# Two down products moved behind the first later unit's difference products, and differences made from the high part

## The chip, the cores and the metric

The kernel runs on one core of one Trainium2 chip. The metric is the device time of one execution in microseconds; of several runs the median is given. The engines are called TensorE (PE in the profile; PEld is its weight load), VectorE (DVE), ScalarE (ACT), GpSimd (POOL) and SyncE (SP, which here only issues DMAs).

## What is computed

The reference is an attention block with a polynomial sketch, followed by a gated feed-forward block:

```python
# 4 batches, 4 heads, 1088 positions, head size 32, sketches of 8
def phi(x):                                  # 64 features per position
    a = einsum('rd,bhsd->bhsr', S1, x); b = einsum('rd,bhsd->bhsr', S2, x)
    return einsum('bhsi,bhsj->bhsij', a, b).reshape(..., 64)
q_p, k_p = phi(q), phi(k)
kv  = einsum('bhsf,bhsd->bhfd', k_p, v);  z = k_p.sum(axis=2)
x   = einsum('bhsf,bhfd->bhsd', q_p, kv) / (einsum('bhsf,bhf->bhs', q_p, z) + 1e-6)
x   = x.transpose(0, 2, 1, 3).reshape(4352, 128)      # tokens x model width
g   = x @ w_gate;  val = x @ w_val                    # 128 x 1536 each
out = (g * sigmoid(g) * val) @ w_out                  # 1536 x 128
```

## The kernel before

**Blocks, units, downs.** The 4352 tokens are cut into blocks: three for batch 0 (384, 384 and 320 columns), then blocks of 480 and a last one of 384. The hidden width of 1536 is cut into twelve chunks of 128. A *unit* is one block and one chunk: its gate and value products, the SiLU and the product of the two, written to a slot of `hbuf` or `late`. A *down* product multiplies one such slot by a chunk of `w_out` and adds into the block's PSUM bank; after twelve of them the bank is transposed (L1117) and stored.

**Two kinds of units.** The three blocks of batch 0 (the *first batch*) use plain 32-bit products (L1027). The *later units*, numbered y = 0 to 83 in `line`, use a split: each operand is cut into a high part (`x1`, the number times `CUT`, rounded), a low part (`x0`, the number less `x1`) and a *difference* (`xd`), and three faster fp32r products take the place of the plain one. `start_unit(y)` issues the two difference products of a unit (L990, one for the gate, one for the value) into a pair of PSUM banks, and one ScalarE instruction that rescales both banks in place (L993). `finish_unit(y)` adds the high and the low products on top (L1003 and L1004, twice each), then ScalarE takes the SiLU (L1006) and VectorE the product (L1011), which frees the pair. There are three pairs. The loop starts unit y + 1 before it finishes unit y, so that a unit's L993 lies beside the products of the unit before; unit 0 is started ahead of the loop.

**The moving side's parts.** `cut_tokens` makes x1 on ScalarE (L882), x0 (L883, on VectorE for the first block and on GpSimd for the six others) and xd on VectorE (L887). `cut_hidden` does the same for the hidden side of 30 chosen down products, in three steps put into later units: the high part h1 at y + 1 (L965 or L967), the low part h0 on GpSimd at y + 2 (L968), the difference hd on VectorE at y + 3 (L971). In the kernel before, both differences are made from the low and the high part: high − 4096 × low.

```python
        nc.vector.scalar_tensor_tensor(
            out=xd[:, 0:n], in0=whole(x0[:, 0:n]), scalar=-BETA, in1=whole(x1[:, 0:n]),
            op0=ALU.mult, op1=ALU.add,
        )
```

The scales in L938 (the plain downs' weights where a block mixes both kinds), L993 and L1096 (the sum of a block's two banks) take the factor 4096 out again.

**Order.** Every engine works off its own instructions in the order in which the program issues them; the order round the change is written out by hand. After the units of batch 0 a loop issues the down products that are left in `todo`, three a turn, and between them pieces of the attention of the later batches (`parts_of`, which takes the next step of the generator `attentions`) and of the cutting of the gate weights (`take`). Then the first later block is cut, and the loop over the later units begins:

```python
    while todo:
        for _ in range(min(3, len(todo))):
            down()
        ...
        parts_of(1 + (begun[0] and len(todo) > 2))
    ...
    run(x_steps or cut_tokens(HEAD, nc.vector))
```

The attention pieces that follow are, one a unit, the transposes of k (L330, two) and of q (L581, two) on VectorE; the groups of small attention products on TensorE (L391, L357, L720, later L345, L783) are called by `group` at y = 4, 6, 20, 22 and 40. `bank()` hands out PSUM banks: by name, in turn, or, once `oldest` is set, the bank that was used longest ago.

Of the kernel before, what the change touches and what calls it, by code (L numbers as in the profile page):

```python
# [12 lines left out]
AF = mybir.ActivationFunctionType  # L13
ALU = mybir.AluOpType
# [5 lines left out]
def kernel(  # L20
# [28 lines left out]
    nc = tc.nc  # L49
# [42 lines left out]
    place = dict(g0=0, g1=1, g2=2, acc=3, a=4, b=6)  # L92
    used = {i: 0 for i in range(8)}
    held = set()
    oldest = [False]
    clock = [0]

    def touch(*which):
# [4 lines left out]
    def hold(*tags):  # L103
        for t in tags:
            held.update((place[t], place[t] + 1) if t in "ab" else (place[t],))
# [7 lines left out]
    def bank(tag=None):  # L113

        if tag is not None:
            i = place[tag]
        elif oldest[0]:
            i = min((i for i in used if i not in held), key=used.get)
        else:
            i = place[free_banks[turn[0] % len(free_banks)]]  # L120
            turn[0] += 1
        touch(i)
        return PS[:, i, :]
# [31 lines left out]
    wo = const.tile([P, NCH, D], FP32, name="wo")  # L155
# [32 lines left out]
    def load_next():  # L188
# [36 lines left out]
        out=ident[:], in_=ident[:], pattern=[[-1, P]], base=0, channel_multiplier=1,  # L225
# [79 lines left out]
    def run(*gens):  # L305
        for g in gens:
            for _ in g:
                pass
# [497 lines left out]
    acc = {}  # L806
    todo = []
# [6 lines left out]

    BETA = 4096.0
    CUT = 1.0 - 2.0**-13
    w_parts = {}
    x_parts = {}  # L820

    def whole(ap):
        return ap.bitcast(FP32)
# [17 lines left out]
    def cut_weights(w, lows, engine):  # L841
# [3 lines left out]
        for c, (w1, wb, wd) in enumerate(homes(w)):  # L845
# [4 lines left out]
            if engine is nc.vector:  # L850
                fine = dict(
                    out=wd, in0=low, scalar=-BETA, in1=whole(w1), op0=ALU.mult, op1=ALU.add
                ), engine.scalar_tensor_tensor
            for row, f, args in zip(
                rows,
                (nc.scalar.activation, engine.tensor_tensor, nc.scalar.activation, fine[1]),
                (
                    dict(out=w1, in_=src, func=AF.Copy, scale=CUT),
                    dict(out=low, in0=src, in1=whole(w1), **sub),
                    dict(out=wb, in_=low, func=AF.Copy, scale=BETA),  # L860
                    fine[0],
# [12 lines left out]
    def cut_tokens(i, engine=nc.gpsimd):  # L874

        t0, n = blocks[i]
        x = xT[:, t0 : t0 + n]
        x1, x0, xd = x_parts[i] = [
            apool.tile([P, WB], F32R, tag=tag, name=name, bufs=2)
            for tag, name in (("qb", "x1"), ("dT", "x0"), ("rd", "xd"))  # L880
        ]
        nc.scalar.activation(x1[:, 0:n], x, AF.Copy, scale=CUT)  # L882
        engine.tensor_tensor(  # L883
            out=x0[:, 0:n], in0=x, in1=whole(x1[:, 0:n]), op=ALU.subtract
        )
        yield
        nc.vector.scalar_tensor_tensor(  # L887
            out=xd[:, 0:n], in0=whole(x0[:, 0:n]), scalar=-BETA, in1=whole(x1[:, 0:n]),
            op0=ALU.mult, op1=ALU.add,
        )  # L890

# [7 lines left out]
    before, behind = {}, {}  # L901

    def add_to(where, y, f):
        where.setdefault(y, []).append(f)
# [5 lines left out]
    def cut_down():  # L910

        n = len(FINE)
        parts = const.tile([P, 3, n, D], F32R, tag="room", name="dparts", bufs=1)
        w1, wb, wd = (parts[:, k] for k in range(3))
        scaled = apool.tile([P, len(PLAIN), D], FP32, tag="zs", name="scaled")
        low = const.tile([P, n, D], FP32, tag="late", name="dlow", bufs=1)
        down_parts.update(w1=w1, wb=wb, wd=wd, scaled=scaled)
        rest = [(0, slice(0, 1)), (1, slice(1, 8, 2)), (5, slice(6, 7)), (6, slice(NCH - 1, NCH))]

        def high(c):  # L920
            nc.scalar.activation(w1[:, c], wo[:, FINE[0] :][:, c], AF.Copy, scale=CUT)

        def left(c):
            nc.gpsimd.tensor_tensor(
                out=low[:, c], in0=wo[:, FINE[0] :][:, c], in1=whole(w1[:, c]), op=ALU.subtract
            )

        def scale(c):
            nc.scalar.activation(wb[:, c], low[:, c], AF.Copy, scale=BETA)

        def differ(c):
            nc.gpsimd.tensor_tensor(
                out=wd[:, c], in0=whole(w1[:, c]), in1=whole(wb[:, c]), op=ALU.subtract
            )

        def other(k, c):
            m = len(range(NCH)[c])
            nc.scalar.activation(scaled[:, k : k + m, :], wo[:, c, :], AF.Copy, scale=-BETA)  # L938

        a, b, c = slice(0, 3), slice(3, 6), slice(6, n)  # L940
        for step in (
            [(high, a)], [(left, a), (high, b)], [(left, b), (scale, a)], [(differ, a), (high, c)],
            [(left, c), (scale, b)], [(differ, b), (scale, c)], [(differ, c), (other, *rest[0])],
            [(other, *rest[1])], [(other, *rest[2]), (other, *rest[3])],
        ):
            for f, *args in step:
                f(*args)
            yield

    def cut_hidden(y, i, j):  # L950

        if not h_sets:
            x = []
            for tag in ("kld", "qld", "vld", "kT", "qT"):
                t = const.tile([P, 2, WB], F32R, tag=tag, name="h" + tag, bufs=1)
                x += [t[:, k, :] for k in range(2)]
            t = const.tile([P, 8, WB], F32R, tag="late", name="hlate", bufs=1)
            x += [t[:, k, :] for k in range(8)]
            h_sets.extend(x[k : k + 3] for k in range(0, 18, 3))
        n = blocks[i][1]  # L960
        h_sets.append(h_sets.pop(0))
        h1, h0, hd = h_parts[i, j] = [x[:, 0:n] for x in h_sets[-1]]
        h = hidden[i, j][:, 0:n]
        if j in (2, 5, 8, 10) and i != line[2]:
            add_to(before, y + 1, lambda: nc.vector.tensor_scalar(h1, h, CUT, None, op0=ALU.mult))  # L965
        else:
            add_to(behind, y + 1, lambda: nc.scalar.activation(h1, h, AF.Copy, scale=CUT))  # L967
        add_to(before, y + 2, lambda: nc.gpsimd.tensor_tensor(  # L968
            out=h0, in0=h, in1=whole(h1), op=ALU.subtract
        ))  # L970
        add_to(before, y + 3, lambda: nc.vector.scalar_tensor_tensor(  # L971
            out=hd, in0=whole(h0), scalar=-BETA, in1=whole(h1), op0=ALU.mult, op1=ALU.add
        ))


# [1 line left out]

    WHOLE = 1.0 + 1.0 / BETA  # L980
    sums_of = {}

    def start_unit(y):

        i, j = line[y // NCH], y % NCH
        n = blocks[i][1]
        xd = x_parts[i][2][:, 0:n]
        ps = sums_of[y] = pair(y)[:, :, 0:n]
        for k, w in enumerate((wg, wv)):
            nc.tensor.matmul(  # L990
                ps[:, k], w_parts[id(w), j // 3][2][:, j % 3, :], xd, start=True, stop=True
            )
        nc.scalar.activation(ps, ps, AF.Copy, scale=-1.0 / BETA / WHOLE)  # L993

    def finish_unit(y):
        i, j = line[y // NCH], y % NCH
# [88 lines left out]
    def copy_out(y, i, n):  # L1085

        x = fpool.tile([P, WB], FP32, tag="sg", name="sum2", bufs=5)[:, 0:n]
        p = acc[i, "p"][:, 0:n]
        acc[i, "p"] = x
        add_to(behind, y + 1, lambda: nc.scalar.activation(x, p, AF.Copy, scale=1.0 + 1.0 / BETA))  # L1090

    def put_together(y, i, n):

        d, x = acc.pop(i)[:, 0:n], acc.pop((i, "p"))
        acc[i] = x
        add_to(before, y + 1, lambda: nc.vector.scalar_tensor_tensor(  # L1096
            out=x, in0=d, scalar=-1.0 / BETA, in1=x, op0=ALU.mult, op1=ALU.add
        ))
        add_to(before, y + 2, lambda: store(i, n))

# [49 lines left out]
    for h in range(H):  # L1150
# [7 lines left out]
    ps = bank("acc")  # L1158
# [5 lines left out]
        out=s12[:],  # L1164
        in0=sTv.unsqueeze(1).to_broadcast([P, H, 2, R]),
        in1=own[:].unsqueeze(2).unsqueeze(3).to_broadcast([P, H, 2, R]),
        op=ALU.mult,
# [14 lines left out]
    for t, c in zip(("acc", "g1", "g2"), (aside, c0, c1)):  # L1182
        ps = bank(t)
# [3 lines left out]
    n = steps[0][1]  # L1187
# [24 lines left out]
    ps = bank("g0")  # L1212
# [8 lines left out]
    ps = bank("g1")  # L1221
# [71 lines left out]
    for z, (i, j) in enumerate(seq):  # L1293
# [16 lines left out]
        if z == 20:  # L1310
# [4 lines left out]
            first, low, second, third = cut_weights(wv, lows, nc.gpsimd)  # L1315
# [19 lines left out]
                take(gates[row], 4 // len(at))  # L1335
    todo.sort()
    x_steps = None
    while todo:
        for _ in range(min(3, len(todo))):
            down()  # L1340
        if len(todo) < 9:
            take(gates[3], 2)
        if begun[0] and not x_steps:
            x_steps = cut_tokens(HEAD, nc.vector)
            run(x_steps)
        parts_of(1 + (begun[0] and len(todo) > 2))
    while not begun[0]:
        parts_of(1)
    run(x_steps or cut_tokens(HEAD, nc.vector))

    flat = hbuf[:].rearrange("p s w -> p (s w)")
    slots[:] = [flat[:, WB * k : WB * k + WB] for k in range((NH - NL) * BW // WB)]
# [7 lines left out]
    for m, i in enumerate(line[1:], 1):  # L1360
        gen = cut_tokens(i)
        for at in {1: (3, 8), 2: (20, 21), 3: (27, 32), 4: (40, 42)}.get(m, (NCH * m - 10, NCH * m - 9)):
            token_steps.setdefault(at, []).append(gen)
    oldest[0] = True
    hold("acc")
    down_steps = cut_down()
    start_unit(0)
    for y in range(END):
        if y in GROUPS:
            group()  # L1370
# [15 lines left out]
    ps = wide("a")[:, 0, 0:D]  # L1386
# [7 lines left out]
    b, x0 = divmod(t0 // 32, NX)  # L1394
# [34 lines left out]
```

## Time and profile before

| | us |
|---|---|
| median of 3 runs (lowest, highest) | 279.7 (279.58, 279.81) |
| the profiled execution's own time | 279.4 |
| its span, first to last instruction | 277.7 |
| TensorE busy (matmuls) | 270.8 |
| VectorE busy | 204.0 |
| ScalarE busy | 184.6 |
| GpSimd busy | 98.8 |

The mean granted clock of TensorE is 0.998 of full speed. The numbers of times and rows come from one profiled execution; its span is 1.7 us shorter than its own time. A row of the timeline gives the start in us from the beginning of the span, the length, the engine, the line of the kernel, the operation with its output and inputs, and in brackets how long the engine stood idle before it and which instruction ended that. A 32-bit matmul shows as two rows of the trace, an fp32r one as a single row. A matmul's row also contains the time that it spends in the pipeline, so that rows overlap: what a product takes is read from one start to the next.

### The profile page before, as it was taken

How to read it: one execution, taken by the hardware profiler on the slowest of the kernel's cores; microseconds unless marked ns; L12 is line 12 of the kernel's file. 1: busy time of each engine (PE TensorE's matmuls, PEld its weight loads, DVE VectorE, ACT ScalarE, POOL GpSimd, SP SyncE). 2: the span in 40 equal slices, each digit the busy share in tenths (PEclk: the TensorE clock that was granted, in tenths of full speed). 3: DMA queues.
4: the chain of work that ended last, by engine and by line, in shares of the span. 5: the costliest groups of instructions: out<-in, count | busy, mean ns of one | idle time of the engine just before them, and what ended most of it. 6: DMA issues, size and time to landing. Idle time of an engine off the chain costs nothing.

```text
span 277.7 us, 5659 instructions
## 1 busy us (share of the span) xinstructions
PE 270.8 (98%) x2169; PEld 197.8 (71%) x2169; DVE 204.0 (73%) x355; ACT 184.6 (66%) x330; POOL 98.8 (36%) x110
## 2 busy tenths in 40 slices
PE   7899999999999999999999999999999999999995
PEld 6545565666756687677577777867887888788994
DVE  3997987976689863787645767967977995987431
ACT  3468566555511586667478898769879878886860
POOL 3314422179820540070034353435335453542000
PEclk9999999999999999999999999999999999999999
DMA  6673195222051123000200020000100200010011
GB/s 191 169 228 88 38 284 176 80 83 77 19 113 28 27 83 96 2 1 0 35 14 5 0 39 0 0 2 9 27 0 2 35 0 0 12 27 0 11 28 28
DMA packets 26140, 14.30 MB, mean 51 GB/s; under 512 B 19841, under 2 KB 24193, under 8 KB 26113
## 3 DMA queue, kind: packets, MB, share of 16 engines
q1 hardware_dynamic: 25456, 13.84, 19.3%
q8 instruction: 17, 0.28, 0.4%
q10 hardware_dynamic: 656, 0.10, 0.2%
q14 instruction: 11, 0.08, 0.1%
HBM read 11.41 MB, written 2.23 MB: 49 GB/s over the span
## 4 chain that ended last, share of the span: by engine, by line
PE 94%; DVE 2%; DMA 1%; ACT 1%; issue 0%; SPq 0%
PE PS L1075 22%; PE PS L1027 16%; PE PS L1003 13%; PE PS L990 13%; PE PS L1004 13%; PE PS L1067 2%; PE PS L1070 2%; PE PS L1069 2%; PE PS L357 2%; PE PS L783 2%; PE PS L345 2%; PE PS L391 2%; DMA kld<-in_k_dram 1%; PE PS L1103 1%; PE PS L500 1%; PE PS L448 1%
## 5 line engine op out<-in xcount | busy, mean ns | idle before, releaser
L993 ACT ACTIVATE PS<-PS 128x960 f32<-128x960 f32 (+1 forms) x84 | 78.4, 935 | 32.8 <-PE PS L990 32.1
L1011 DVE SCALAR_TENSOR_TENSOR hbuf<-PS,sg 128x480 f32<-128x480 f32 (+1 forms) x84 | 53.7, 639 | 43.8 <-ACT sg L1006 43.2
L1006 ACT ACTIVATE sg<-PS 128x480 f32<-128x480 f32 (+1 forms) x84 | 46.7, 556 | 2.0 <-PE PS L1004 1.3
L990 PE MATMUL PS<-xd,gphq 128*128 128x480 f32 (+1 forms) x84 | 47.1, 561 | 0.0
L1075 PE MATMUL PS<-hbuf,wo 128*128 128x480 f32 (+3 forms) x118 | 45.9, 492 | 0.0
L1003 PE MATMUL PS<-x,graw 128*128 128x480 f32 (+1 forms) x84 | 32.1, 382 | 0.6 <-ACT PS L993 0.6
L1004 PE MATMUL PS<-x,wb 128*128 128x480 f32 (+1 forms) x84 | 31.6, 376 | 0.0
L990 PE MATMUL PS<-xd,wd 128*128 128x480 f32 (+1 forms) x84 | 31.4, 374 | 0.0
L1003 PE MATMUL PS<-x,w 128*128 128x480 f32 (+1 forms) x84 | 31.4, 374 | 0.0
L1004 PE MATMUL PS<-x,graw 128*128 128x480 f32 (+1 forms) x84 | 31.3, 373 | 0.0
L1027 PE MATMUL PS<-xT,wg 128*128 128x384 f32 (+1 forms) x72 | 28.7, 480 | 0.1
L1027 PE MATMUL PS<-xT,wv 128*128 128x384 f32 (+1 forms) x72 | 28.0, 471 | 0.2 <-DVE wv L289 0.2
L1075 PEld LDWEIGHTS PS<-hbuf,wo 128*128 128x128 f32 x118 | 22.1, 189 | 7.4 <-issue 0.9
L1031 ACT ACTIVATE sg<-PS 128x384 f32<-128x384 f32 (+1 forms) x30 | 13.8, 465 | 18.7 <-PE PS L1027 17.0
L990 PEld LDWEIGHTS PS<-xd,gphq 128*128 128x128 f32 x84 | 15.8, 188 | 9.9 <-ACT PS L993 6.4
L990 PEld LDWEIGHTS PS<-xd,wd 128*128 128x128 f32 x84 | 15.8, 189 | 9.7 <-issue 6.2
L883 POOL TENSOR_TENSOR x<-xT,x 128x480 fp32r<-128x480 f32 (+1 forms) x6 | 7.1, 1179 | 38.2 <-ACT x L882 38.2
L1027 PEld LDWEIGHTS PS<-xT,wv 128*128 128x128 f32 x72 | 13.4, 190 | 8.9 <-DVE hbuf L1042 0.9
L1027 PEld LDWEIGHTS PS<-xT,wg 128*128 128x128 f32 x72 | 12.9, 189 | 9.3 <-issue 1.2
L1003 PEld LDWEIGHTS PS<-x,graw 128*128 128x128 f32 x84 | 15.7, 187 | 4.4 <-ACT PS L993 1.6
L1075 PE MATMUL PS<-hbuf,scaled 128*128 128x480 f32 x36 | 17.4, 565 | 0.0
L1003 PEld LDWEIGHTS PS<-x,w 128*128 128x128 f32 x84 | 15.8, 188 | 2.2
(184 smaller groups left out, 492.7 us busy)
## 6 DMA issues: line engine op xcount, KB each, us to landing
kld<-in_k_dram SPq DMA_DIRECT2D x4, 544.0 KB, 4.1
vld<-in_v_dram SPq DMA_DIRECT2D x12, 144.0 KB, 4.7
qld<-in_q_dram SPq DMA_DIRECT2D x3, 544.0 KB, 3.3
raw<-in_moe_w_out_dram SPq DMA_DIRECT2D x4, 384.0 KB, 4.0
raw<-in_moe_w_gate_dram SPq DMA_DIRECT2D x3, 384.0 KB, 3.2
raw<-in_moe_w_val_dram SPq DMA_DIRECT2D x3, 384.0 KB, 3.6
out_dram<-o SPq DMA_DIRECT2D x16, 60.0 KB, 2.0
vld<-in_v_dram SPq DMA_DIRECT2D x4, 112.0 KB, 4.4
```

What stands on the lines that cost most here:

```text
L345: nc.tensor.matmul(ps[32 * a : 32 * a + 32, 96 * (c - c0) : 96 * (c - c0) + 96], qT[:, 4 * c + a, :], s123[:, a : a + H, :, :].rearrange(" ...
L357: nc.tensor.matmul(ps[32 * a : 32 * a + 64, 64 * (c - c0) : 64 * (c - c0) + 64], kT[:, c, a : a + 2, :].rearrange("p a t -> p (a t)"), s12 ...
L883: engine.tensor_tensor(out=x0[:, 0:n], in0=x, in1=whole(x1[:, 0:n]), op=ALU.subtract)
L990: nc.tensor.matmul(ps[:, k], w_parts[id(w), j // 3][2][:, j % 3, :], xd, start=True, stop=True)
L993: nc.scalar.activation(ps, ps, AF.Copy, scale=-1.0 / BETA / WHOLE)
L1003: nc.tensor.matmul(ps[:, k], w1, x1, start=False, stop=False, skip_group_check=True)
L1004: nc.tensor.matmul(ps[:, k], wb, x0, start=False, stop=True, skip_group_check=True)
L1006: nc.scalar.activation(sg, ps[:, 0], AF.Silu, scale=WHOLE)
L1011: nc.vector.scalar_tensor_tensor(out=hj[:, 0:n], in0=ps[:, 1], scalar=WHOLE, in1=sg, op0=ALU.mult, op1=ALU.mult)
L1027: nc.tensor.matmul(o[:, 0:n], w[:, j, :], xT[:, t0 : t0 + n], start=True, stop=True)
L1031: nc.scalar.activation(sg[:, 0:n], g[:, 0:n], AF.Silu)
L1075: nc.tensor.matmul(acc[i][:, 0:n], w, hidden[i, j][:, 0:n], **sides)
```

## The change

It does four things. The differences are made from the high part and the number itself: xd = x1 × (1 + 1/4096) − x, which is the old one divided by 4096; hd likewise. The scales that took out the 4096 become −1 or lose the factor. For the first later block, where all parts are made on VectorE, the difference comes ahead of the low part. The loop over the left-over downs stops at two; `start_unit(0)` is issued then, and the two downs (the last two of batch 0's third block, 320 columns) follow behind its difference products. The rule of the bank used longest ago is taken out. `WHOLE` is 1 + 1/4096, as before, only defined earlier.

```diff
@@ bank
-        elif oldest[0]:
-            i = min((i for i in used if i not in held), key=used.get)
@@ cut_tokens
         nc.scalar.activation(x1[:, 0:n], x, AF.Copy, scale=CUT)
-        engine.tensor_tensor(
-            out=x0[:, 0:n], in0=x, in1=whole(x1[:, 0:n]), op=ALU.subtract
-        )
+        def low():
+            engine.tensor_tensor(
+                out=x0[:, 0:n], in0=x, in1=whole(x1[:, 0:n]), op=ALU.subtract
+            )
+        def difference():
+            nc.vector.scalar_tensor_tensor(
+                out=xd[:, 0:n], in0=whole(x1[:, 0:n]), scalar=WHOLE, in1=x,
+                op0=ALU.mult, op1=ALU.subtract,
+            )
+        first, second = (difference, low) if engine is nc.vector else (low, difference)
+        first()
         yield
-        nc.vector.scalar_tensor_tensor(
-            out=xd[:, 0:n], in0=whole(x0[:, 0:n]), scalar=-BETA, in1=whole(x1[:, 0:n]),
-            op0=ALU.mult, op1=ALU.add,
-        )
+        second()
@@ cut_down, other
-            nc.scalar.activation(scaled[:, k : k + m, :], wo[:, c, :], AF.Copy, scale=-BETA)
+            nc.scalar.activation(scaled[:, k : k + m, :], wo[:, c, :], AF.Copy, scale=-1.0)
@@ cut_hidden
-            out=hd, in0=whole(h0), scalar=-BETA, in1=whole(h1), op0=ALU.mult, op1=ALU.add
+            out=hd, in0=whole(h1), scalar=WHOLE, in1=h, op0=ALU.mult, op1=ALU.subtract
@@ start_unit
-        nc.scalar.activation(ps, ps, AF.Copy, scale=-1.0 / BETA / WHOLE)
+        nc.scalar.activation(ps, ps, AF.Copy, scale=-1.0 / WHOLE)
@@ put_together
-            out=x, in0=d, scalar=-1.0 / BETA, in1=x, op0=ALU.mult, op1=ALU.add
+            out=x, in0=d, scalar=-1.0, in1=x, op0=ALU.mult, op1=ALU.add
@@ the loop over the left-over downs, and what follows it
-    while todo:
-        for _ in range(min(3, len(todo))):
+    while len(todo) > 2:
+        for _ in range(min(3, len(todo) - 2)):
             down()
...
     run(x_steps or cut_tokens(HEAD, nc.vector))
+    hold("acc")
+    start_unit(0)
+    while todo:
+        down()
...
-    oldest[0] = True
-    hold("acc")
     down_steps = cut_down()
-    start_unit(0)
     for y in range(END):
```

More of the change, by code (lines that the diff above doesn't have):

```diff
@@ L94 @@
     held = set()
-    oldest = [False]
     clock = [0]
@@ L818 @@
     CUT = 1.0 - 2.0**-13
+    WHOLE = 1.0 + 1.0 / BETA
     w_parts = {}
@@ L971, in cut_hidden @@
         add_to(before, y + 3, lambda: nc.vector.scalar_tensor_tensor(
-            out=hd, in0=whole(h0), scalar=-BETA, in1=whole(h1), op0=ALU.mult, op1=ALU.add
+            out=hd, in0=whole(h1), scalar=WHOLE, in1=h, op0=ALU.mult, op1=ALU.subtract
         ))
     room = const.tile([P, 10, BW], FP32, tag="room", name="room", bufs=1)
-    WHOLE = 1.0 + 1.0 / BETA
     sums_of = {}
@@ L1089, in copy_out @@
         acc[i, "p"] = x
-        add_to(behind, y + 1, lambda: nc.scalar.activation(x, p, AF.Copy, scale=1.0 + 1.0 / BETA))
+        add_to(behind, y + 1, lambda: nc.scalar.activation(x, p, AF.Copy, scale=WHOLE))
     def put_together(y, i, n):
```

## The prediction

> **What bounds the kernel now.** I read the page's busy shares first, then the chain that ended last, then TensorE's own waits, then the timeline round the one wait that the change can reach.
>
> Busy shares and the chain: TensorE is busy for 98% of the span and makes 94% of the chain. A change is worth only what it takes out of TensorE's idle time, or out of its list of products, and no product is added or removed here.
>
> ```profile
> PE 270.8 (98%) x2169; PEld 197.8 (71%) x2169; DVE 204.0 (73%) x355; ACT 184.6 (66%) x330; POOL 98.8 (36%) x110
> PE 94%; DVE 2%; DMA 1%; ACT 1%; issue 0%; SPq 0%
> ```
>
> All waits of TensorE's matmuls (engine, line, what for, total us, times, longest): six in the whole run, and only one falls into the part that the change touches.
>
> ```profile
> PE PS L357 <- DVE kT L330: 0.9, 1, 0.9
> PE PS L244 <- PEq L1413: 0.9, 1, 0.9
> PE PS L1003 <- ACT PS L993: 0.6, 1, 0.6
> ```
>
> The timeline round it (start, length, engine, line; TensorE's lines, then ScalarE's, then VectorE's):
>
> ```profile
> 88.72 3.93 PE L1075 MATMUL PS<-late,wo 128*128 128x320 f32 x14
> 92.25 0.62 PE L990 MATMUL PS<-xd,gphq 128*128 128x480 f32 x1
> 92.71 0.38 PE L990 MATMUL PS<-xd,wd 128*128 128x480 f32 x1
> 92.93 0.38 PE L990 MATMUL PS<-xd,gphq 128*128 128x480 f32 x1
> 93.15 0.37 PE L990 MATMUL PS<-xd,wd 128*128 128x480 f32 x1
> 94.14 0.48 PE L1003 MATMUL PS<-x,graw 128*128 128x480 f32 x1 [0.61 <-ACT PS L993]
> 94.46 0.38 PE L1004 MATMUL PS<-x,graw 128*128 128x480 f32 x1
> ...
> 93.13 1.82 ACT L993 ACTIVATE PS<-PS 128x960 f32<-128x960 f32 x2 [3.50 <-PE PS L990]
> ...
> 89.79 0.65 DVE L883 TENSOR_TENSOR x<-xT,x 128x480 fp32r<-128x480 f32 x1
> 90.47 0.66 DVE L887 SCALAR_TENSOR_TENSOR xd<-x,x 128x480 fp32r<-128x480 f32 x1
> ```
>
> The first batch's last down products run into the difference products of units 0 and 1 (four L990). Then ScalarE must rescale unit 0's sums (L993) before L1003 may add to them. ScalarE starts at 93.13, when unit 0's second L990 is complete, and TensorE resumes at 94.14. Neighbouring products start 0.22 us apart (92.93 to 93.15), so without the wait L1003 would start at 93.37 and L1004 at 93.58. L1004 starts at 94.46: **0.88 us are lost**, 0.77 of it ahead of L1003 and 0.1 as the pipe refills.
>
> **What the Trainium skill says.** "TensorE: Matmul & The Clock Gate", section "What overlaps and what doesn't" under "The mechanism", has matmuls start and end strictly in program order; the trace agrees: nothing passes the waiting L1003, so only a product placed ahead of it fills the hole. "ScalarE: Activation LUTs", section "What ACT_TABLE_LOAD costs", prices an ACTIVATE with immediates at 186 ns + 0.833 ns an element, 986 ns for 960, with 93 ns of overlap; the trace has 935 ns on average, and 0.86 us from one start to the next. "SBUF — State Buffer", section "Who interferes with whom": a VectorE instruction with two SBUF inputs and a GpSimd one that reads SBUF shut each other out; L971 (two SBUF inputs) takes from 609 to 1678 ns here, which agrees.
>
> **The change, part by part.**
>
> *Two down products behind unit 0's difference products.* Eight downs of 320 columns stood ahead (two rows each, 16 rows); six stay, and the last two, four rows, now follow unit 0's two L990. A row takes (3.93 − 0.43)/13 = 0.27 us, so four take 1.07 us. All TensorE work up to L1003 is the same; its order is not:
> - Unit 0's L990 start 1.07 us earlier, at 91.18 and 91.64 by the rows' starts.
> - ScalarE's L993 starts 1.07 us earlier, 93.13 → 92.06, ends about 93.0 and lets L1003 go at 93.07 (94.14 − 1.07).
> - TensorE fills that time with the four rows, then unit 1's two L990, and comes to L1003 at 93.37 as before without a wait. 93.37 is 0.30 us past 93.07: the wait is gone and 0.88 us with it.
> - The mixing itself: units with one 480-column down run at 2.12 us, those without at 1.31 us, and the down's own two rows take 0.81 (the chain's "0.81 PE PS L1075 x2"), so a change of product kind costs 0.00 to 0.02 us. I take zero.
>
> What is late next? L990(0) needs xd. The 14 rows of 0.27 us from 88.72 keep TensorE to 92.48, so the first L990 streams then whatever its row says; 1.07 earlier is 91.41, and xd was ready at 91.13. The block's store (L1117) waits for the last down, now near 93.1; VectorE reaches it at 93.72, behind the phk products, as before, so the store's DMAs on SP go out when they did. No queue's DMAs change their order.
>
> *xd from x1 and x, ahead of x0, for the first block.* Same two operations, same inputs in SBUF: 0.65 and 0.66 us swapped. xd is ready at 90.45 instead of 91.13. Gain zero: the downs cover it, and 0.28 us would have been left even without the swap. x0 is needed by L1004, at 93.58, and is ready at 91.1.
>
> *Six later xd and 30 hd from the high part.* VectorE's instructions are as many and as large. The wait for GpSimd's low part goes: of VectorE's instructions 32 wait for GpSimd instead of 47, and the view of VectorE's waits has no row with GpSimd as releaser: the low part was always there already. Zero, with bounds: below, a gain of up to 0.2 us (the smallest row of that view); above, see the port rival. New waits stand at TensorE's L1004 (for VectorE's x0, long done) and at some L1011 (for GpSimd's earlier read of a reused slot, units ago): the next instruction there is one that waits for ScalarE anyway. Zero. The scales −1 for −4096 in L938, L993 and L1096 are immediates of the same instructions: zero.
>
> *Side effect on the generator of attention pieces.* The shorter loop takes one piece less, so on VectorE each kT and qT transpose (0.80, 0.70, 0.83, 0.70 us) moves behind the L1011 it stood ahead of. Queued behind them are the L1011 of units 1 to 3, which free PSUM pairs for L990 of units 4 to 6. Unit 0's L1011 can start near 94.95 (ScalarE's SiLU from 94.43), ends 95.6; kT ends 96.4, just as unit 1's SiLU does. L1011 of unit 1 ends about 97.10, and L990 of unit 4 needs it: 97.14 against 97.95 before. So 0.81 of the 0.88 are carried past there. The second kT ends at 97.7 and its readers (L357) start near 99.5; the second qT ends about 100.6, for L345 at 104.6. POOL's sums end at 99.21 whatever happens, for L720 at 100.7. The load of the next q goes out some 0.7 us later, with 5 us to spare.
>
> *The freest-bank rule removed.* In the later units every bank is asked for by name, and TensorE's order shows no other change. Zero.
>
> **Sum:** 0.88 at most and 0.81 past unit 4; I take the middle, **−0.85 us**. Behind unit 4 TensorE sets the pace (2.12 us a unit) to the end, so the shift reaches the end. The profiled execution took 279.4 us for a span of 277.7; it becomes 278.55 for 276.85. The median of the runs is 279.7, 0.3 above it: **278.85 us**. A difference of 0.2%, 0.56 us, is about what a measurement of this kernel can tell from none; 0.85 is 0.30%.
>
> **The rivals.**
> - *Half is given back in units 1 to 3.* ScalarE needs 0.86 + 0.46 = 1.32 us a unit where TensorE needs 1.31, and my working leaves L1003 of units 1 and 2 under 0.1 us of slack; VectorE's kT leaves none. Three waits of 0.1 to 0.15 us take 0.3 to 0.45 back: 279.2 to 279.3. For it: the equal rates. Against: ScalarE had 0.24 us idle before unit 2's L993 and keeps it. Chance 0.16.
> - *More than the hole.* If freeing VectorE from GpSimd's results also shortens waits of PE for L1011 (1.0 us in all for L990, four times), 0.3 more comes: 278.5. Chance 0.06.
> - *Slower: the shared port.* Without the semaphore on h0, L971 could start while GpSimd's low parts run, and be shut out: 1.4 us instead of 0.64. In 188 to 250 us VectorE is busy 52.3 of 62; 13 more blocked rows at 0.75 us use the rest up, and from two more on the 0.85 is lost. If all 16 rows that are now short were blocked, 16 × 0.75 = 12 us overfill the stretch by 2.4: 281.2. Against: VectorE did not wait for h0, so nothing starts earlier. Chance 0.08.
> - *It does not do what it says:* the order of TensorE does have the two downs behind L990, so this is left out.
>
> **How the numbers follow.** Main case 0.70, 278.65 to 279.05. Faster = main and "more", 0.76; same = half given back, 0.16; slower 0.08. The range 278.4 to 279.6 takes in the first two rivals.
>
> **What would show it.** Right: the wait of L1003 for L993 at 94 us gone or under 0.1; between the first L990 and L1004 of unit 0 four L1075 rows; L1004 of unit 0 at 93.6; L990 of unit 4 near 97.1; the last L1103 0.85 earlier; L971's mean unchanged (about 1.0 us). Wrong: a new PE or PEld wait for L993 or L1011 between 94 and 99; L971 longer, with VectorE full from 188 to 250; a shift that shrinks at the group of attention products near 100, 137 or 184.

## The result, and the profile after

| | before | after |
|---|---|---|
| median of 7 runs each, us | 279.69 (279.42 to 279.81) | 278.80 (278.63 to 278.95) |
| profiled execution: own time / span, us | 279.4 / 277.7 | 278.89 / 277.2 |
| ratio of the times, 95% interval | | 0.997 [0.9958, 0.9981] |

The change makes the kernel faster by 0.3%: 0.89 us by the medians. The forecast was 278.85, or −0.85 us. A few executions of most kernels take over 1 us longer than the rest, and the ratios below are worked out from all executions, so they differ from the quotients of the medians by up to 0.0006.

The line numbers of the changed kernel have moved. The rows that matter: difference products L990 → L997, their rescaling L993 → L1000, high and low products L1003/L1004 → L1010/L1011, SiLU L1006 → L1013, VectorE's product L1011 → L1018 (so "L1011" is TensorE's low product from here on, where the kernel has the change), downs L1075 → L1082, hd L971 → L979, kT L330 → L327, the first group of attention products L391 → L388, the last products of the program L1103 → L1110.

First the page of the changed kernel: busy times and the chain's shares by engine. TensorE is still the bound, at 98% of the span and 94% of the chain.

```profile
PE 271.4 (98%) x2169; PEld 198.3 (72%) x2169; DVE 203.7 (74%) x355; ACT 184.5 (67%) x330; POOL 98.9 (36%) x110
PE 94%; DVE 2%; DMA 2%; ACT 1%; issue 0%; SPq 0%
```

Second, all waits of TensorE's matmuls in the changed kernel (line, what for, total us, times, longest). The wait of the high product for ScalarE's rescaling, 0.6 us before, has no successor: no row names L1010 or L1000 (rescaling).

```profile
PE PS L241 <- PEq L1421: 0.9, 1, 0.9
PE PS L354 <- DVE kT L327: 0.4, 1, 0.4
PE PS L497 <- ACT kvz L1230: 0.4, 1, 0.4
PE PS L412 <- ACT kvs L1227: 0.3, 1, 0.3
PE PS L1034 <- DVE wv L286: 0.2, 1, 0.2
```

The weight load (PEld) waits ahead of its product, and shows more. From 90 to 98 us it has these waits, the kernel before first and then the changed one:

```profile
PEld PS L1003 <- ACT PS L993: 1.0, 1, 1.0
PEld PS L990 <- DVE hbuf L1011: 0.2, 1, 0.2
```

```profile
PEld PS L997 <- issue: 0.3, 1, 0.3
PEld PS L1010 <- ACT PS L1000: 0.2, 1, 0.2
```

Before, these are unit 0's high product and unit 4's second difference product. After, they are unit 3's second difference product, for which the profile names no releaser, and unit 1's high product: the wait for the rescaling is gone at unit 0, and a small one has come up at unit 1.

Third, the timeline of the changed kernel round the edit (start, length, engine, line, count; TensorE's rows, then ScalarE's, then VectorE's; what stands in brackets is the idle time ahead of a row and who ended it).

```profile
88.96 2.86 PE L1082 MATMUL PS<-late,wo 128*128 128x320 f32 x10
91.42 0.62 PE L997 MATMUL PS<-xd,gphq 128*128 128x480 f32 x1
...
92.09 1.24 PE L1082 MATMUL PS<-late,wo 128*128 128x320 f32 x4
...
93.61 0.38 PE L1010 MATMUL PS<-x,graw 128*128 128x480 f32 x1
93.83 0.38 PE L1011 MATMUL PS<-x,graw 128*128 128x480 f32 x1
...
94.92 0.45 PE L1010 MATMUL PS<-x,graw 128*128 128x480 f32 x1
95.20 0.38 PE L1011 MATMUL PS<-x,graw 128*128 128x480 f32 x1
...
95.85 0.38 PE L997 MATMUL PS<-xd,gphq 128*128 128x480 f32 x1
96.14 0.46 PE L997 MATMUL PS<-xd,wd 128*128 128x480 f32 x1
96.44 0.38 PE L1010 MATMUL PS<-x,graw 128*128 128x480 f32 x1
...
98.71 1.21 PE L388 MATMUL PS<-phk,vld 128*32 128x64 f32 x72
...
92.29 0.95 ACT L1000 ACTIVATE PS<-PS 128x960 f32<-128x960 f32 x1 [2.41 <-PE PS L997]
93.87 0.95 ACT L1000 ACTIVATE PS<-PS 128x960 f32<-128x960 f32 x1 [0.62 <-PE PS L997]
94.74 0.57 ACT L1013 ACTIVATE sg<-PS 128x480 f32<-128x480 f32 x1
...
95.33 0.66 DVE L1018 SCALAR_TENSOR_TENSOR hbuf<-PS,sg 128x480 f32<-128x480 f32 x1 [0.98 <-ACT sg L1013]
95.91 0.83 DVE L327 STREAM_TRANSPOSE kT<-kld 128x640 f32<-128x640 f32 x1
```

Four rows of downs (92.09, x4) stand between unit 0's and unit 1's difference products, and L1010 follows at 93.61 with no wait. ScalarE starts to rescale at 92.29, beside those four rows. But ScalarE then idles 0.62 us (93.24 to 93.87), because unit 1's difference products come only behind both downs. TensorE, too, has three small breaks: from 94.92 to 95.20, from 95.85 to 96.14 and from 96.14 to 96.44 are 0.28 to 0.30 us where neighbours start 0.22 apart. The first two are the two waits of the weight load above. The third stands behind the second as the 0.32 us between L1003 and L1004 (94.14 to 94.46) stood behind the wait of the kernel before.

**One clock for all kernels.** The spans of single profiles are not compared directly, since the first load of k lands at a different moment in each. I count from the start of the last run of `late` downs (88.72 before, 88.96 after) to the first group of attention products, which TensorE reaches behind units 0 to 4, and to the last x16 row of L1103/L1110 in the chain. Before, the group in the timeline and the last row of the chain are

```profile
99.21 1.21 PE L391 MATMUL PS<-phk,vld 128*32 128x64 f32 x72
...
272.63 1.80 PE PS L1103 x16
```

After, the chain has

```profile
1.26 4.35 DMA kld<-in_k_dram
...
6.27 1.49 PE PS L354 x36
...
272.12 1.80 PE PS L1110 x16
```

The table looks ahead to the experiments e1 to e7 of the next section. In its last column, each median has beside it the median of the kernel before that was measured together with it.

| kernel | downs to group, us | against before | downs to last products | against before | median (before) |
|---|---|---|---|---|---|
| before | 10.49 | | 183.91 | | |
| after | 9.75 | −0.74 | 183.16 | −0.75 | 278.80 (279.69) |
| e1: the order alone | 9.74 | −0.75 | 183.11 | −0.80 | 278.84 (279.62) |
| e2: the differences alone | 10.49 | 0.00 | 183.87 | −0.04 | 279.58 (279.62) |
| e3: one down moved | 9.92 | −0.57 | 183.28 | −0.63 | 279.10 (279.62) |
| e4: one down, and one | 9.62 | −0.87 | 182.99 | −0.92 | 278.62 (279.62) |
| e5: kT put back | 9.74 | −0.75 | 183.17 | −0.74 | 278.78 (279.46) |
| e6: a useless product | 10.48 | −0.01 | 183.92 | +0.01 | 279.48 (279.46) |
| e7: e4 and a down ahead of a group | 9.59 | −0.90 | 183.65 | −0.26 | 279.25 (279.46) |

In the changed kernel 0.74 us is gained by the first group, and it stays to the end: −0.75. There is one profile of each kernel; those that ought to agree (after, e1 and e5; before, e2 and e6) do so within 0.01 us at the group and 0.06 us at the end. The profiled spans differ by only 0.5 us because k landed 0.27 us later in the profile of after (4.35 against 4.08).

### The profile page after: what moved, and what is told of

Read it like the earlier page. It is cut to its first block, busy times and chain, and to the rows that moved or that the text cites. A ratio compares the mean times of both kernels' runs of the same rounds, so it can differ in the third digit from the quotient of the medians.

```text
span 277.2 us, 5670 instructions
## 1 busy us (share of the span) xinstructions
PE 271.4 (98%) x2169; PEld 198.3 (72%) x2169; DVE 203.7 (74%) x355; ACT 184.5 (67%) x330; POOL 98.9 (36%) x110
## 4 chain that ended last, share of the span: by engine, by line
PE 94%; DVE 2%; DMA 2%; ACT 1%; issue 0%; SPq 0%
PE PS L1082 22%; PE PS L1034 16%; PE PS L1010 13%; PE PS L997 13%; PE PS L1011 13%; PE PS L1074 2%; PE PS L1077 2%; PE PS L1076 2%; PE PS L354 2%; PE PS L780 2%; PE PS L342 2%; PE PS L388 2%; DMA kld<-in_k_dram 2%; PE PS L1110 1%; PE PS L497 1%; PE PS L445 1%
## 5 line engine op out<-in xcount | busy, mean ns | idle before, releaser
L1000 ACT ACTIVATE PS<-PS 128x960 f32<-128x960 f32 (+1 forms) x84 | 78.5, 935 | 32.0 <-PE PS L997 31.2
L1018 DVE SCALAR_TENSOR_TENSOR hbuf<-PS,sg 128x480 f32<-128x480 f32 (+1 forms) x84 | 53.7, 640 | 43.6 <-ACT sg L1013 40.8
L1013 ACT ACTIVATE sg<-PS 128x480 f32<-128x480 f32 (+1 forms) x84 | 46.7, 556 | 2.0 <-PE PS L1011 1.2
L997 PE MATMUL PS<-xd,gphq 128*128 128x480 f32 (+1 forms) x84 | 47.3, 564 | 0.0
L1082 PE MATMUL PS<-hbuf,wo 128*128 128x480 f32 (+3 forms) x118 | 45.9, 492 | 0.0
L1010 PE MATMUL PS<-x,graw 128*128 128x480 f32 (+1 forms) x84 | 32.1, 382 | 0.0
L1011 PE MATMUL PS<-x,wb 128*128 128x480 f32 (+1 forms) x84 | 31.6, 376 | 0.0
L997 PE MATMUL PS<-xd,wd 128*128 128x480 f32 (+1 forms) x84 | 31.4, 374 | 0.0
L1010 PE MATMUL PS<-x,w 128*128 128x480 f32 (+1 forms) x84 | 31.4, 374 | 0.0
L1011 PE MATMUL PS<-x,graw 128*128 128x480 f32 (+1 forms) x84 | 31.3, 373 | 0.0
L1082 PEld LDWEIGHTS PS<-hbuf,wo 128*128 128x128 f32 x118 | 22.1, 189 | 7.4 <-issue 0.9
L997 PEld LDWEIGHTS PS<-xd,gphq 128*128 128x128 f32 x84 | 15.8, 188 | 10.0 <-ACT PS L1000 6.4
L997 PEld LDWEIGHTS PS<-xd,wd 128*128 128x128 f32 x84 | 15.8, 189 | 9.9 <-issue 6.7
L1010 PEld LDWEIGHTS PS<-x,graw 128*128 128x128 f32 x84 | 15.7, 187 | 3.5 <-ACT PS L1000 0.8
L1082 PE MATMUL PS<-hbuf,scaled 128*128 128x480 f32 x36 | 17.4, 565 | 0.0
L1010 PEld LDWEIGHTS PS<-x,w 128*128 128x128 f32 x84 | 15.8, 188 | 2.2
```

The source lines that it names most:

```text
L997: nc.tensor.matmul(ps[:, k], w_parts[id(w), j // 3][2][:, j % 3, :], xd, start=True, stop=True)
L1000: nc.scalar.activation(ps, ps, AF.Copy, scale=-1.0 / WHOLE)
L1010: nc.tensor.matmul(ps[:, k], w1, x1, start=False, stop=False, skip_group_check=True)
L1011: nc.tensor.matmul(ps[:, k], wb, x0, start=False, stop=True, skip_group_check=True)
L1013: nc.scalar.activation(sg, ps[:, 0], AF.Silu, scale=WHOLE)
L1018: nc.vector.scalar_tensor_tensor(out=hj[:, 0:n], in0=ps[:, 1], scalar=WHOLE, in1=sg, op0=ALU.mult, op1=ALU.mult)
```

## The experiments

**e1 and e2: the two halves of the change.** e1 is the kernel before with the new order alone; the differences, their scales and the order x0, xd stay as they were:

```diff
-    while todo:
-        for _ in range(min(3, len(todo))):
+    while len(todo) > 2:
+        for _ in range(min(3, len(todo) - 2)):
...
     run(x_steps or cut_tokens(HEAD, nc.vector))
+    hold("acc")
+    start_unit(0)
+    while todo:
+        down()
...
-    oldest[0] = True
-    hold("acc")
     down_steps = cut_down()
-    start_unit(0)
```

> Only the order of the change: the loop stops at two left-over downs, unit 0 is started, the two downs follow. All differences are made from the low part as before, x0 ahead of xd. Theory (the hole before L1003 was filled, and nothing else counts): as the whole change, 0.8 to 0.9 us under the kernel before, about 278.8; xd is ready at 91.1, 0.3 us ahead of its first L990, so the old order of x0 and xd costs nothing. Rival (the differences from the high part bring a share): less than the whole change by that share, and L990 of unit 0 waits for xd.

e2 is the changed kernel with the order put back (`oldest[0] = True` stays out), so that only the differences, with the swap of x0 and xd, and the scales are new. The rule of the bank used longest ago is thus out in both. It was idle in the kernel before: only the units of batch 0 call `bank()` without a name, and they are all issued before the rule is set.

> Only the differences and their scales: made from the high part and the number itself, xd ahead of x0 for the first block, but all left-over downs ahead of unit 0 as in the kernel before. Theory: 0.0 us, 279.7 (within 0.15 us), with the wait of L1003 for L993 back at 0.6 us in TensorE's waits and 1.0 in the weight load's. Rival one (VectorE freed from GpSimd's results shortens later waits): 0.2 us or more faster. Rival two (the shared port): slower, with L971's rows longer than 1.0 us on average.

Measured: e1 278.84, ratio 0.9976 [0.9967, 0.9986]; e2 279.58, ratio 0.9996 [0.9983, 1.0009]. TensorE's weight load in e2, 90 to 98 us, has the old wait again:

```profile
PEld PS L1010 <- ACT PS L1000: 1.0, 1, 1.0
```

The order is the whole gain. The new source of the differences and the swap of x0 and xd are worth nothing that can be measured, in either direction: e2 differs from before by 0.00 us at the group, and after from e1 by 0.01.

**e3 and e4: how many downs, and where.** e3 leaves one down more ahead of `hold("acc")` (a line `down()`), so that only one follows unit 0's difference products. e4 puts one behind unit 0's and the other behind unit 1's:

```diff
-    while todo:
-        down()
+    down()
...
             start_unit(y + 1)
+        if y == 0:
+            down()
+            slots.pop()
```

(`slots.pop()` keeps the slot which that last down gives back, cut for 320 columns, out of the new list.)

> As the changed kernel, but one down instead of two stands behind unit 0's difference products. Theory (the hole is filled by what is put into it): unit 0's L993 is let go 0.54 us earlier than in the kernel before instead of 1.07, at 93.6 on its clock; TensorE gets to L1003 at 93.37, so 0.23 us of wait and the refill of 0.1 stay: 0.54 us faster than before, 279.15; the weight load's wait for L993 is near 0.45. Rival (what counts is that unit 0 starts before the last down at all, or a fixed cost of the change of product kind): as the whole change, 278.8.

> As the changed kernel, but of the two downs one stands behind unit 0's difference products and one behind unit 1's. In the changed kernel unit 1's L993 starts 0.62 us after the one before has ended, because unit 1's L990 stand behind both downs; that makes unit 0's SiLU and VectorE's product late, and TensorE loses 0.06 at L1003 of unit 1, 0.08 and 0.08 at L990 and L1003 of units 3 and 2. Theory: here unit 1's L993 follows at once (0.6 us earlier than in the changed kernel), those small waits go, 0.1 to 0.2 us faster than the changed kernel: 278.65. Rival (ScalarE's rate of 1.32 us a unit sets it, whatever the order): the same as the changed kernel, 278.8, and the waits stay. Second rival: with one down only ahead of unit 1 the wait of L1003 for L993 of unit 0 comes back (0.2 us or more).

Measured: e3 279.10, ratio 0.9988 [0.9976, 1.0]; e4 278.62, ratio 0.9964 [0.9953, 0.9976], the lowest median of all the kernels, though its interval overlaps that of the change. In e3 the weight load still waits, in 90 to 98 us:

```profile
PEld PS L1010 <- ACT PS L1000: 0.5, 1, 0.5
```

One down is two rows, 0.54 us; e3 gains 0.57 by the first group. So the gain is the filled hole: what is put in is gained, until the hole is full. The timeline of e4 (TensorE, then ScalarE):

```profile
91.89 0.70 PE L1082 MATMUL PS<-late,wo 128*128 128x320 f32 x2
...
92.86 0.70 PE L1082 MATMUL PS<-late,wo 128*128 128x320 f32 x2
93.16 0.62 PE L1010 MATMUL PS<-x,graw 128*128 128x480 f32 x1
...
98.38 1.21 PE L388 MATMUL PS<-phk,vld 128*32 128x64 f32 x72
...
92.09 1.99 ACT L1000 ACTIVATE PS<-PS 128x960 f32<-128x960 f32 x2 [2.42 <-PE PS L997]
94.09 0.57 ACT L1013 ACTIVATE sg<-PS 128x480 f32<-128x480 f32 x1
```

Both rescalings now run without a gap (one row, x2), the SiLU of unit 0 starts 5.33 us behind the first down (94.09 − 88.76) where the change has 5.78 (94.74 − 88.96), and at the places of the three small breaks neighbours start 0.21 to 0.22 us apart. The gain at the group is 0.87 us of the 0.88 that were lost.

**e5: is it kT?** The prediction blamed a part of the loss on kT, which stands behind VectorE's product in the changed kernel. e5 takes one attention piece right after the moved downs, which puts kT and qT ahead again:

```diff
     while todo:
         down()
+    parts_of(1)
```

> As the changed kernel, but one piece of the attention is taken behind the two downs, so that each kT and qT transpose stands ahead of the L1011 (the product of a unit) again as in the kernel before. It tests the term of the prediction that a kT behind unit 0's L1011 makes unit 1's late. Theory: the first kT fits into VectorE's 0.98 us of idle time before unit 0's L1011; the waits of 0.06 and 0.08 come from unit 0's SiLU, not from kT, and stay: TensorE's time from its first left-over down of the slots in late to the small products of the first group differs by under 0.05 us from the changed kernel's 9.75; 278.8. Rival (the transposes' place costs what is missing from the 0.88): 0.1 us and more less, near 9.62, and 278.7 or less.

Measured: 278.78, ratio 0.9975 [0.9968, 0.9983], 9.74 us to the group against 9.75. VectorE in e5:

```profile
94.20 0.80 DVE L327 STREAM_TRANSPOSE kT<-kld 128x640 f32<-128x640 f32 x1
95.24 0.66 DVE L1018 SCALAR_TENSOR_TENSOR hbuf<-PS,sg 128x480 f32<-128x480 f32 x1 [0.24 <-ACT sg L1013]
```

kT is back where it was, and L1018 of unit 0 starts 6.35 us behind the first down, against 6.37 after: it waits for the SiLU either way. kT is not the cause.

**e6: is a product in the hole free?** The kernel before, with one extra product of a down's size between the difference products of units 0 and 1:

```diff
     start_unit(0)
+    nc.tensor.matmul(
+        bank("g2")[:, 0:320], wo[:, 0, :], xT[:, 0:320], start=True, stop=True
+    )
```

> The kernel before with one product more that nothing reads: 320 columns, 32-bit, into a bank that is free then, between the difference products of unit 0 and those of unit 1, where the changed kernel has its downs. All downs stay ahead. Theory (TensorE has 0.77 us there that nothing uses): the 0.54 us of the useless product cost nothing, 279.6, and TensorE's wait at L1003 shrinks from 1.0 to about 0.45 (weight load). Rival (TensorE's rate is what counts, or the wait moves along): 0.5 us slower, 280.15.

Measured: 279.48, ratio 1.0001 [0.9993, 1.0009], and 10.48 us to the group against 10.49. The timeline of TensorE in e6, and the weight load's wait (before's line numbers; the extra product is L1368):

```profile
92.99 0.70 PE L1368 MATMUL PS<-xT,wo 128*128 128x320 f32 x2
...
94.20 0.48 PE L1003 MATMUL PS<-x,graw 128*128 128x480 f32 x1
```

```profile
PEld PS L1003 <- ACT PS L993: 0.5, 1, 0.5
```

Two rows more and no time more: L1003 starts 5.41 us behind the first down (94.20 − 88.79), before it was 5.42. Until L993 is done TensorE's time is free there, and the wait shrinks by what is put into it.

**e7: the same at another group?** In e4 the weight load also waits 0.6 us at unit 40, where the L780 products need VectorE's product of the unit before:

```profile
PEld PS L780 <- DVE hbuf L1018: 0.6, 1, 0.6
```

e7 is e4 with a queued down moved into that place, and the queue kept one shorter from there on:

```diff
+        if y == 40:
+            down(y)
         if y in GROUPS:
             group()
...
-            if len(todo) > min(5 + (todo[0] == (line[1], 0)), END - y + 1):
+            if len(todo) > min((5 if y < 40 else 4) + (todo[0] == (line[1], 0)), END - y + 1):
```

> The one-each kernel with the same thing done at a second hole: the group of attention products at unit 40 waits until VectorE has freed unit 39's pair of banks; TensorE stands about 0.75 us there. One left-over down is issued ahead of that group, and from unit 40 on the queue of left-over downs is kept at four instead of five, so that each later unit keeps its down. Theory: the down's 0.81 us cover the wait; but the first down of the next block, one unit earlier too, now waits up to 0.45 us for ScalarE's copy of that bank (L1090 of the kernel before). So 0.3 to 0.7 us faster than one-each, 277.9 to 278.3. Rival (later the shorter queue makes VectorE's hd late for its product, or the bank's copy takes all of it back): 278.6 or slower, with new waits of TensorE behind 184 us.

Measured: 279.25, ratio 0.9998 [0.9991, 1.0004]. That is slower than e4, as the rival had it, and not faster. On the downs' clock 0.90 us is gained by the first group and 0.26 at the end: most of e4's gain is gone. The timelines of TensorE round unit 40, e4 first and then e7:

```profile
182.87 2.26 PE L780 MATMUL PS<-phT,spread 32*32 32x288 f32 x64
185.06 0.48 PE L1010 MATMUL PS<-x,graw 128*128 128x480 f32 x1
```

```profile
182.68 0.97 PE L1082 MATMUL PS<-hbuf,scaled 128*128 128x480 f32 x2
183.57 1.57 PE L780 MATMUL PS<-phT,spread 32*32 32x288 f32 x64
185.07 0.49 PE L1010 MATMUL PS<-x,graw 128*128 128x480 f32 x1
...
186.96 1.07 PE L1082 MATMUL PS<-hbuf,scaled 128*128 128x480 f32 x2 [0.30 <-ACT sum L1097]
```

The moved down itself is nearly free: L1010 of unit 40 starts 96.42 us behind the first down of `late` (185.07 − 88.65), in e4 96.30 (185.06 − 88.76), so that 0.81 us of product cost 0.12. But the queue is now one ahead for good, so the next down is the first of the next block, and it must wait for ScalarE's copy of the bank (L1097), which runs from 186.34 to 186.90. The waits of the weight load in e7, 178 to 278 us, show that one and three more of 0.4 us, which e4 does not have:

```profile
PEld PS L1076 <- DVE sum L1103: 0.8, 2, 0.4
PEld PS L1082 <- ACT sum L1097: 0.7, 1, 0.7
PEld PS L1074 <- DVE hqT L979: 0.4, 1, 0.4
```

L1076 waits twice for VectorE's sum of a block's two banks (L1103 in this kernel's numbers), so again for a bank that is not free yet. L1074 waits for an hd that VectorE makes too late, which the rival had named. At the end e7 is 0.66 us behind e4 (183.65 against 182.99). That this comes from the shorter queue, rather than from the moved down alone, was not separated: the two edits were tried together only.

## Why the prediction was right, and where a term was mis-sized

On the downs' clock, step by step:

| step | predicted | measured |
|---|---|---|
| start of unit 0's high product | −0.77 | 5.42 → 4.65 us: −0.77 |
| start of unit 0's low product | −0.88 | 5.74 → 4.87: −0.87 |
| second difference product of unit 4 | −0.81 | 9.23 → 8.56: −0.67 |
| first group, and the end | −0.85 | −0.74, and −0.75 |

*The hole.* Right, in its size, its cause and its price of 0.27 us a row: e3 and e6 put two of the four rows into it, one with useful and one with useless work.

*Mixing the kinds of products.* Taken as zero, and zero: the low product gains 0.87 of 0.88 although TensorE changes kind twice more.

*xd from the high part; the swap; the scales.* Zero by e2 and e1.

*The shared port (the slower rival).* It didn't occur. L979 of the changed kernel, in its largest group (count, busy us, mean ns, idle ahead), has the mean that L971 had before, 1100 ns:

```profile
L979 DVE SCALAR_TENSOR_TENSOR hlate<-hlate,hbuf 128x480 fp32r<-128x480 f32 x10 | 11.0, 1100 | 0.0
```

All 30 of them together take 30.4 us, as before. The timelines of both kernels show what makes some of them long: the 14 rows over 1 us all start while a GpSimd instruction is under way, and none of the 16 rows under 0.7 us does.

*The side effect on kT: the mis-sized term, 0.81 past unit 4 by the working where 0.67 was measured.* The time named for VectorE was right: the second L1018 ends at 97.34, and 97.10 was predicted on before's clock, which stands 0.24 us earlier. But TensorE came to unit 4 later than that, behind the three breaks before it. The working left two things unpriced: L1010 of units 1 and 2 had "under 0.1 us of slack" and was put at zero, and unit 3's second difference product, which needs unit 0's L1018, wasn't looked at, only unit 4's. In the timeline L1018 ends at 95.99 and that product starts at 96.14. And the blame on kT was wrong: e5 moves kT back and changes nothing. What delays SiLU(0), L1018(0) and the products behind them is that unit 1's difference products stand behind *both* downs, so ScalarE idles 0.62 us; e4 takes one down out of its way and has 0.87.

*The rival "half is given back".* It had the place right and the size too large: the three breaks take 0.20 us back by unit 4, from 0.87 to 0.67, instead of 0.3 to 0.45. The weight load's new wait for L1000 at unit 1, 0.2 us, is one of the signs that the prediction had named for being wrong; it came, but small. By the first group 0.07 us returns (0.74), because the kernel before has a break of its own behind unit 4's second difference product, from 97.95 to 98.25, where the changed kernel has 0.21 us (97.52 to 97.73). The prediction did not see that one either.

*Readings.* The 935 ns for a rescaling mix 72 instructions of 960 elements with 12 of 768; those of 960 take 0.95 to 0.98 us in the timelines here, which is closer to the price worked out beside it. The range from 609 to 1678 ns is that of one group of L971; over its five groups it reaches 1703. And 12 us exceed the 9.7 that VectorE had left by 2.3, not by 2.4. Nothing in the sum rests on these.

*The total.* Its mechanism is right, and its size to about 0.1 us. The medians' 0.89 us (0.997 with its interval means 0.53 to 1.17) can't tell 0.75 from 0.85; the traces can. So it is in part luck that the median came within 0.05 us of the forecast: 0.75 us under 279.69 would be 278.94.

## What to carry to other kernels

When a product waits for another engine's result, put independent work between the two, but count that work also against the *next* link: what stands behind it in program order may be what feeds the other engine. Filler split so that the other engine never idles (one down behind each start, e4) recovered 0.87 of the 0.88 us; both behind the first recovered 0.74. And work that is taken from a queue to fill a hole can run the queue ahead from there on: in e7 the hole took 0.81 us of work for 0.12, and then the next block's first down waited for a bank that wasn't free yet.

## What the runs showed of the hardware that was not expected

The first load of k takes a different time from profile to profile, 4.07 to 4.94 us here. In the two profiles in which it was longest, the first products behind it ran slower. In e2 the head of the chain is

```profile
1.26 4.49 DMA kld<-in_k_dram
6.41 2.19 PE PS L354 x36
```

where before and after had 4.08 and 4.35 us and 1.49 us for the same 36 products. In e2 the load takes 0.4 us longer than before, and the downs start 1.5 us later (90.25 against 88.72); the profiled execution of e2 took 280.89 us where its median is 279.58. e3's profile (4.94 and 2.19 us) is the same case, with the downs at 90.49. Why the 36 products are slower then wasn't tested. The length of TensorE's wait ahead of them does not decide it: before waited 0.9 us for k's transpose and then took 1.49 us, e2 waited 0.4 us and took 2.19. For changes of a few tenths of a microsecond it means that two profiles are compared from a common event behind the head, not by their spans.
